# The channel MLP's first two rows computed whole, and its order of products rewritten, in an attention and MLP kernel

## The chip, the core and the metric

The kernel runs on one core of a Trainium2 chip. Its engines are TensorE (PE, with PEld for its weight loads), VectorE (DVE), ScalarE (ACT), GpSimd (POOL) and SyncE (SP, which issues the transfers). The metric is the device time of one execution in microseconds.

## The reference

```python
attn = softmax(q @ k.T / sqrt(D) + bias) @ v                # 4 batches, 8 heads, 576 tokens, 64 wide
x = attn, heads side by side                                # (4, 576, 512)
h = relu(x.T @ w_tok1) @ w_tok2;  u = x + h.T               # token MLP, 256 hidden
y = u + relu(u @ w_ch1) @ w_ch2                             # channel MLP, 1536 hidden
u2, v2 = split(gelu(y @ w_in))                              # gated MLP
out = y + (u2 * (w_sg @ norm(v2) + b_sg)) @ w_out
```

The change is in the channel MLP, and in the last steps of the token MLP ahead of it.

## The kernel before

A float32 operand is split into a high and a low part: ACT copies it to fp32r (the high part), DVE subtracts that from the operand (the low part). A product is three matmuls, high by high, high by low and low by high. X holds the activations, 512 channels in four blocks of 128 by 2304 tokens.

The channel MLP takes the tokens in three parts: tokens 0 to 1023 (pass 0, `d0`), the 256 tokens from 1024 on, along with pass 0 (`up256`, `down256`), and the last 1024 (pass 1, `d1`). The 1536 hidden channels are 12 blocks f, two to a row j. A row is a product of 2x2 blocks: two hidden blocks by two halves of the channels, times two halves of the channels by two halves of 512 tokens. It is computed with seven block products in place of eight, from sums of weight blocks (`wsum`, S1 to S4, made in four pieces by `sum_steps`) and sums of activation blocks, the mixers M1 to M4 and M22. A block product (`product`) is 6 matmuls of 512 columns. The products of a row are here called P1 (bank a, first half of wa by first half of u), P2 (bank b), S2M2 (onto a), S1M1 (bank c), S3M3 (onto a), P4 (M4, onto a), P3 (S4M22, onto c). Each time before bank a is accumulated onto again, ACT copies what it holds (to s1, then c12, then c22, the last two in `slots`). The other four outputs of a row go through relu into g tiles (`gs`, two) and then into the down product with w_ch2 (`down`, 12 matmuls of 512 columns into four banks a0 to a3): `down1` for the first 512 tokens of the pass row by row, and for the other 512 once every two rows, for both rows ("others", four down products) after which `add_up` adds the banks to X on DVE. A row that begins a new pair (rows 2 and 4) carries the others of the pair before it; the last pair's come in a closing part after row 5.

Row 0 of pass 0 is special (`first`): its first output, the relu of pg, is computed whole in the token stage with 12 matmuls; the row then needs six products more.

Weights come as 512 KB transfers into two buffers, and are turned into float32 and split by a queue of jobs (`Jobs`). A job has four pieces: ACT squares one word, DVE does L159, L165, L170 and L175; its high part is copied by ACT in the second piece of the next job and its low part subtracted by DVE in the third (`finish`, `subtract`). In pass 0 each row has five jobs: wa, wq with wb, the row's sums, and two of w_ch2, called c. `work(k)` runs k pieces, `step(k)` runs k pieces, one entry of `builds` (mixers for pass 1), pending low parts of relus and one transposing of the residual (`rfill`). `need` runs as many pieces as it takes for a weight to be ready. `wjobs.limit` holds the queue back until buffers are free. In pass 1 all weights of w_ch1 come back split from memory, and the queue turns the next stage's weights.

All orders are written out by hand; every engine takes its instructions in the order in which the program writes them, and waits where a semaphore tells it to. `bank(nm)` gives one of eight PSUM banks: ma, mb, mx, my and a0 to a3.

Of the kernel before, what the change touches and what calls it, by code (L numbers as in the profile page):

```python
# [19 lines left out]
def kernel(ctx, tc, ins, consts, out, dbg=None, nb=4, stop=None):  # L20
# [5 lines left out]
    P = 128  # L26
# [1059 lines left out]
    if True:  # L1086
# [23 lines left out]
        for b in range(nb):  # L1110
# [19 lines left out]
            for d in range(ND):  # L1130
                next_x(b + 1, d + 1, xs)
                tok2(b, d, h)
                if b == nb - 1 and d < 2 * ND2:
                    b11, b12, b21, b22 = [x[:, d % ND2] for x in quarters(0)]
                    t = tk.tile([P, NS - d % 2, DM], F32, tag=f"x{d % 2}", name="raw")[:, 0]
                    if d < ND2:
                        raw_sum(t, b12, b11)
                        split_to(M1, d, t)
                    else:
# [79 lines left out]
    with tc.tile_pool(name="ps_ch", bufs=1, space=PSUM, reuse_waits="tile") as pc:  # L1219
# [7 lines left out]
        def down(acc, g, f, start, stop):  # L1227
            wjobs.need(("c2", f))
            for d in range(ND):
# [11 lines left out]
        builds, pending = [], []  # L1241
# [12 lines left out]

        def up256(j):

            wjobs.need(("c1", 2 * j + 1))
            pg = bank("mx")
# [8 lines left out]
            relu(pg, gs[0])  # L1267
# [20 lines left out]
        class Double:  # L1288
# [13 lines left out]
            def down1(self, j, e, group):  # L1302
                if self.acc is None:
                    self.acc = new_acc()
                down(self.acc, gs[e], 2 * j + e, j == group[0] and e == 0, j == group[-1] and e == 1)
# [13 lines left out]
            def others_down(self, acc, lst, k):  # L1319
# [4 lines left out]
            def run(self, hooks, first=False, small=False, banks=("mb", "mb"), end=None):  # L1324

                self.small = small
                seq = [(g, j) for g in self.groups for j in g]
                for n, (group, j) in enumerate(seq):
                    pgrp, pj = seq[n - 1] if n > 0 else (None, None)
                    begins = n > 0 and j == group[0]  # L1330
                    direct = first and n == 0
# [5 lines left out]
                    sm = small and n < len(seq) - 1  # L1337
                    hooks(n, "start")
                    a = bank("ma")
                    product(a, self.half(w_a, 0), self.half(self.u, 0), start=True)  # L1340
                    if not direct:
                        S.copy(out=s1, in_=a)
                    step(self.pieces)
                    if direct:
                        self.down1(j, 0, group)
                    elif n > 0 and not (first and n == 1):
                        self.down1(pj, 0, pgrp)
# [3 lines left out]
                    step(self.pieces)  # L1351
                    if begins:
                        self.down1(pj, 1, pgrp)
                        self.close()
                        self.second(0, lst)
                        step(self.pieces)
                    if not direct:
                        b = bank(banks[0])
                        product(b, self.half(w_a, 1), self.half(self.u, 1), start=True)
                        V.tensor_tensor(out=s1, in0=b, in1=s1, op=ALU.add)  # L1360
                    hooks(n, "P2")
                    step(self.pieces)
                    wjobs.need(("sum", j))
                    product(a, ws_(S2), M2)
                    S.copy(out=c12, in_=a)  # L1365
                    step(self.pieces)
                    if sm and n > 0:
                        down256(j)
                    if begins:
                        self.second(1, lst)  # L1370
                    elif not direct:
                        relu(s1, gs[0])
                    step(self.pieces)
                    if begins:
                        acc, h_ = new_acc(), len(lst) // 2
                        for k in range(h_):
                            self.others_down(acc, lst, k)
                            step(self.pieces)
                    c = bank(banks[1])
# [5 lines left out]
                    step(self.pieces)  # L1385
                    if begins:
                        for k in range(h_, len(lst)):
                            self.others_down(acc, lst, k)
                            if not small and k + 2 == len(lst):
                                relu(s1, gs[0])  # L1390
                            if k + 1 < len(lst):
                                step(self.pieces)
                        add_up(acc, self.c0 + CK, range(ND2))
                        if small:
                            relu_hi(s1, gs[0])
                            relu_lo(s1, gs[0])
                        add_up(acc, self.c0 + CK, range(ND2, ND))
# [3 lines left out]
                    elif sm:  # L1401
# [439 lines left out]
```

## Time and profile before

| | us |
|---|---|
| median of 3 runs | 914.03 (913.85 to 915.43) |
| the profiled execution | 914.67, span 912.9 |
| PE, DVE, ACT, POOL busy | 865.9, 703.2, 453.1, 229.3 |
| pass 0 | 359.2 to 563.1 |
| pass 1 | 563.1 to 700.2 |

The span is what the profile covers of the execution. Times in the rows below are in us from its start. A matmul's own duration is longer than the distance to the next one, since matmuls are pipelined; the distance between starts is the pace.

### The profile page before, as it was taken

To read this page: it belongs to the slowest core of one execution; us is meant where nothing else is said; L and a number is where in the kernel's file an instruction comes from. 1 tells how busy PE (TensorE), PEld (TensorE's weight loads), DVE (VectorE), ACT (ScalarE), POOL (GpSimd) and SP (SyncE) were. 2 spreads that over 40 slices of the span, in tenths; PEclk is the share of its full clock that TensorE was granted. 3 is DMA by queue.
4 is the path that set the end of the run, shared out by engine and by line. 5 is a ranking of instruction groups with operands and counts; after the bars stand their busy time and mean duration, and the time that the engine had idled before them with its cause. 6 is when DMAs were issued, how large, how long until landed. Compare 5 with 4: busy or idle time off the path is not lost. (4 is left out here: it accounts for less than half of the span.)

```text
span 912.9 us, 21627 instructions
## 1 busy us (share of the span) xinstructions
PE 865.9 (95%) x8608; PEld 712.3 (78%) x8608; DVE 703.2 (77%) x1531; ACT 453.1 (50%) x993; POOL 229.3 (25%) x440
## 2 busy tenths in 40 slices
PE   9999999999999997888988989999989999999998
PEld 4466788888888886766876767787867999989997
DVE  7899688888887787677767785456485989988856
ACT  7999788888888432333233342123243532323310
POOL 0345576766766000000000000000002232321240
PEclk9999999999999999889999999999989999999999
DMA  7956544444431330135233110325042001000002
GB/s 187 195 125 138 133 79 84 82 88 86 95 77 39 86 113 24 47 104 172 81 116 116 46 47 24 136 84 209 11 107 52 35 24 47 1 34 25 1 13 93
DMA packets 127732, 74.30 MB, mean 81 GB/s; under 512 B 104592, under 2 KB 112912, under 8 KB 126352
## 3 DMA queue, kind: packets, MB, share of 16 engines
q1 hardware_dynamic: 127472, 72.79, 30.1%
q8 instruction: 68, 1.11, 0.5%
q14 instruction: 32, 0.26, 0.1%
q10 hardware_dynamic: 160, 0.13, 0.1%
HBM read 47.01 MB, written 13.11 MB: 66 GB/s over the span
## 5 line engine op out<-in xcount | busy, mean ns | idle before, releaser
L530 POOL TENSOR_SCALAR pr<-pr,sm 128x576 f32<-128x576 f32 (+2 forms) x208 | 129.7, 640 | 47.4 <-DVE sm L523 39.2
L1231 PE MATMUL a<-g,c 128*128 128x512 f32 x528 | 130.9, 401 | 9.2 <-ACT g L1070 5.2
L1231 PEld LDWEIGHTS a<-g,c 128*128 128x128 f32 x528 | 102.0, 195 | 32.8 <-ACT g L1070 5.7
L516 ACT ACTIVATE pr<-pr,mn 128x576 f32<-128x576 f32 x144 | 112.2, 779 | 6.9 <-DVE mn L503 4.6
L503 DVE CUSTOM_DVE_ANT_0 pr<-ss,bias_m 128x576 f32<-128x576 f32 x128 | 94.6, 750 | 19.9 <-PE ss L497 17.0
L63 POOL TENSOR_TENSOR y<-X,y 128x576 fp32r<-128x576 f32 x4 | 5.6, 1426 | 402.5 <-ACT y L62 402.5
L597 PE MATMUL o<-xA,vm 64*64 64x128 f32 (+1 forms) x1280 | 78.8, 261 | 0.0
L597 PEld LDWEIGHTS o<-xA,vm 64*64 64x64 f32 x1280 | 69.9, 133 | 11.1 <-issue 5.4
L1186 DVE STREAM_TRANSPOSE res<-X 32x256 f32<-32x256 f32 (+1 forms) x176 | 68.1, 387 | 2.8
L598 PE MATMUL o<-yA,vm 64*64 64x128 f32 x1024 | 68.0, 272 | 0.0
L497 PE MATMUL ss<-kt,X 64*64 64x288 f32 x816 | 66.8, 410 | 0.0
L598 PEld LDWEIGHTS o<-yA,vm 64*64 64x64 f32 x1024 | 56.3, 133 | 0.3
L1652 PE MATMUL ps<-wsT,vn 128*128 128x288 f32 x384 | 56.4, 295 | 0.0
L374 DVE TENSOR_SCALAR X<-ttab,wsm 128x576 f32<-128x576 f32 x108 | 55.4, 574 | 0.1
L1652 PEld LDWEIGHTS ps<-wsT,vn 128*128 128x128 f32 x384 | 52.7, 188 | 0.3 <-POOL vn L63 0.2
L1630 PEld LDWEIGHTS pu<-y,c 128*128 128x128 f32 x384 | 51.3, 188 | 0.3
L1630 PE MATMUL pu<-y,c 128*128 128x288 f32 x384 | 51.5, 294 | 0.0
L158 ACT ACTIVATE sq<-wraw 128x512 f32<-128x512 f32 (+2 forms) x43 | 27.9, 648 | 41.4 <-DVE w L175 23.4
L573 PE MATMUL x<-ident,pr 128*128 128x128 f32 x320 | 47.0, 273 | 0.0
L1064 PE MATMUL ma<-m,ws 128*128 128x512 f32 x144 | 38.4, 403 | 7.9 <-ACT cs L1365 7.9
L1683 PE MATMUL po<-u,gm 128*128 128x512 f32 x192 | 44.0, 389 | 0.0
L1683 PEld LDWEIGHTS po<-u,gm 128*128 128x128 f32 x192 | 36.0, 188 | 7.4
(239 smaller groups left out, 1975.7 us busy)
## 6 DMA issues: line engine op xcount, KB each, us to landing
wraw<-in_moe_w_ch_dram SPq DMA_DIRECT2D x24, 512.0 KB, 3.7
bias_m<-bst SPq DMA_DIRECT2D x32, 288.0 KB, 4.1
s<-ws SPq DMA_DIRECT2D x5, 1024.0 KB, 4.0
ws<-s SPq DMA_DIRECT2D x5, 1024.0 KB, 5.2
vm<-in_v_dram SPq DMA_DIRECT2D x32, 128.0 KB, 3.1
wraw<-in_moe_w_in_dram SPq DMA_DIRECT2D x8, 512.0 KB, 4.3
out_dram<-res SPq DMA_DIRECT2D x16, 256.0 KB, 2.1
kr<-in_k_dram SPq DMA_DIRECT2D x48, 72.0 KB, 2.7
```

What stands on the lines that cost most here:

```text
L374: V.tensor_scalar(out=hd, in0=tt, scalar1=b1i, scalar2=None, op0=ALU.min)
L497: T.matmul(ss[a % na][o, hf, 0:HN], lhsT=ql, rhs=kr_, start=True, stop=True)
L503: V.tensor_tensor_reduce(out=pr[:, a * NB:a * NB + N].rearrange("p (f n) -> p f n", f=2), in0=ss[a][:, :, 0:HN], in1=bias[a].rearrange("p ...
L516: S.activation(out=pr[:, a * NB:a * NB + N], in_=pr[:, a * NB:a * NB + N], func=AF.Exp, scale=-1.0, bias=mn[:, a:a + 1], accum_out=sm[:, a ...
L530: G.tensor_scalar(out=pr[:, dc:dc + hi - lo], in0=pr[:, lo:hi], scalar1=sm[:, a:a + 1], scalar2=1.0, op0=ALU.mult, op1=ALU.mult,)
L597: T.matmul(o[0:HD, 0:w], lhsT=vm[r, t, 0], rhs=xs[r, t, 0:w], start=st_, stop=en)
L598: T.matmul(o[HD:P, 0:w], lhsT=vm[r, t, 1], rhs=rh[r], start=st_, stop=en)
L1186: V.transpose(out=o, in_=src(c)[32 * a:32 * a + 32])
L1231: T.matmul(acc[d], lhsT=c2[f][i][:, d * P:(d + 1) * P], rhs=g[:, j], start=start and m == 0, stop=stop and m == 2,)
L1630: T.matmul(pu[:, hf, 0:HN], lhsT=wi[i][0][d][:, f * P:(f + 1) * P], rhs=y[j][:, d, js], start=d == 0 and m == 0, stop=d == ND - 1 and m == 2,)
L1652: T.matmul(ps[:, hf, 0:HN], lhsT=vn[i][:, t, ds_], rhs=wsT[j][:, t, js], start=t == 0 and m == 0, stop=False,)
L1683: T.matmul(po[:, cs], lhsT=g[i][:, d, gs], rhs=wo[j][d][:, cs], start=d == 0 and m == 0, stop=d == NG - 1 and m == 2,)
```

## The change

The first two of the twelve rows of hidden blocks, row j = 0 here, are now computed without sums in pass 0: `pair0` makes C12 (bank a), C22 (bank b) and later C21 (bank c) with 12 matmuls each, from the weights and the activations themselves. For that M1 and M2 hold at first the two blocks of u for tokens 512 to 1023, split in the token stage, and the four mixers are built inside `pair0`. The split of the 256 tokens (x256) moves to the token stage. `up256` comes after S2M2 and `down256` after P4, or after the first of the others. A down product can be done in two parts, d 0 and 1, then 2 and 3 (pass 1). The low part of a relu follows at once; only that of the 256 tokens stands apart. In pass 1 bank a is ma and my by turns. Steps have three pieces in pass 0 (two before) and two in pass 1 (three before); builds are called one by one. The split of u0 for the next stage moves from P2 to P4 of the last row.

```diff
-                if b == nb - 1 and d < 2 * ND2:
...
-                        raw_sum(t, b22, b12)
-                        raw_sum(t, t, b11, ALU.add)
-                        split_to(M2, d % ND2, t)
+                if b == nb - 1 and d == 0:
+                    split(quarters(0)[1], *M1)
+                if b == nb - 1 and d == 1:
+                    split(quarters(0)[3], *M2)
+                if b == nb - 1 and d == 2:
+                    x256 = chw.tile([P, 2, ND, CS], F32R, tag="ws1", name="x256")
+                    split(X[:, :, C256:C256 + CS], x256[:, 0], x256[:, 1])
...
         def relu(src, g):
             relu_hi(src, g)
-            pending.append(lambda: relu_lo(src, g))
+            relu_lo(src, g)
 
         def step(k):
             work(k)
-            if builds:
-                builds.pop(0)()
-            while pending:
-                pending.pop(0)()
             rfill(1)
...
+            def other(self, acc, lst, k, n=0):
                 down(acc, self.g(k), lst[k][0], k == 0, k == len(lst) - 1)
                 if k + 2 < len(lst):
                     self.second(k + 2, lst)
+                step(n)
+
+            def pair0(self):
+
+                (j, j1), a, b = self.groups[0], bank("ma"), bank("mb")
+                for ps, w, m in ((a, [wa[j][:, i] for i in range(2)], (M1, M2)), (b, None, (M1, M2))):
+                    for e in range(2):
+                        if w is None:
+                            w2 = [(wq, wb)[e][j][:, i] for i in range(2)]
+                        else:
+                            w2 = self.half(w, e)
+                        product(ps, w2, m[e], start=e == 0)
+                    S.activation(out=slots[0 if w is not None else 1], in_=ps, func=AF.Relu)
+                self.hooks(0, "others")
+                self.down1(j, 0, self.groups[0])
+                up256(j)
+                relu_lo_256()
+                c = bank("ma")
+                for e in range(2):
+                    product(c, [(wq, wb)[e][j][:, i] for i in range(2)], self.half(self.u, e), start=e == 0)
+                relu(c, gs[1])
+                self.hooks(0, "C21")
+                down256(j)
+                self.hooks(0, "P3")
...
+                    k_ = self.pieces
+                    a = bank(banks[n % 2])
                     product(a, self.half(w_a, 0), self.half(self.u, 0), start=True)
+                    S.copy(out=s1, in_=a)
+                    step(k_)
+                    if da:
+                        self.down1(pj, 0, pgrp, range(ND) if small or begins else range(ND2))
+                    step(k_)
+                    if begins:
+                        if not small:
+                            self.second(0, lst)
+                        self.down1(pj, 1, pgrp)
+                        self.close()
+                        if small:
+                            self.second(0, lst)
+                        else:
+                            self.second(1, lst)
+                    b = bank(banks[2])
+                    product(b, self.half(w_a, 1), self.half(self.u, 1), start=True)
+                    V.tensor_tensor(out=s1, in0=b, in1=s1, op=ALU.add)
+                    hooks(n, "P2")
+                    wjobs.need(("sum", j))
+                    product(a, ws_(S2), M2)
+                    S.copy(out=c12, in_=a)
+                    step(k_)
+                    if da and not small and not begins:
+                        self.down1(pj, 0, pgrp, range(ND2, ND))
+                        relu(s1, gs[0])
                     if sm:
                         up256(j)
                         hooks(n, "up")
+                        step(k_ if not begins else 1)
+                        relu_lo_256()
                     if begins:
+                        acc = new_acc()
+                        self.other(acc, lst, 0, k_)
+                        if small:
+                            down256(j)
+                            self.second(1, lst)
+                        else:
+                            self.other(acc, lst, 1, k_)
+                    c = bank(banks[3])
                     product(c, ws_(S1), M1, start=True)
                     product(a, ws_(S3), M3)
                     S.copy(out=c22, in_=a)
                     V.tensor_tensor(out=c22, in0=c, in1=c22, op=ALU.add)
                     hooks(n, "P7")
+                    step(k_)
                     if begins:
+                        for k in range(1 if small else 2, len(lst)):
+                            self.other(acc, lst, k, k_ if k + 1 < len(lst) else 0)
...
+                        add_up(acc, self.c0 + CK)
                         if small:
+                            relu(s1, gs[0])
                         hooks(n, "done")
                     elif n > 0:
                         self.down1(pj, 1, pgrp)
+                        step(1)
                     product(a, [wb[j][:, i] for i in range(2)], M4)
                     relu(a, gs[1])
                     hooks(n, "P4")
+                    if sm and not begins:
+                        down256(j)
+                        relu(s1, gs[0])
+                    elif not sm and not begins and (small or not da):
+                        relu(s1, gs[0])
                     product(c, ws_(S4), M22)
                     V.tensor_tensor(out=c12, in0=c, in1=c12, op=ALU.add)
                     hooks(n, "P3")
...
-        d0.pieces, d1.pieces = 2, 0
+        d0.pieces, d1.pieces = 3, 0
...
+            if n == 0 and where == "others":
+                mixer(3, raws(), 0)
+                for i in range(2):
+                    S.copy(out=M22[i], in_=M2[i].bitcast(F32))
+                mixer(2, raws(), 0)
+            if n == 0 and where == "C21":
+                wjobs.limit = base + 8
+                work(8)
+                mixer(1, slots[2:4], 0)
             if where == "P3":
                 wjobs.limit = base + 5 * (n + 1) + 5
-                work(4)
+                work(4 if n > 0 else 0)
+            if n == 0 and where == "P3":
+                mixer(4, raws(), 0)
...
-                d1.pieces = 3
-            if n == NJ - 1 and where == "P2":
+                d1.pieces = 2
+            if n == NJ - 1 and where == "P4":
                 y0.extend(u_parts(0, u0))
...
-        d1.run(hooks1, banks=("mb", "mx"), end=("mb", "mx", "my", "ma"))
+        d1.run(hooks1, banks=("ma", "my", "mb", "mx"), end=("ma", "mb", "mx", "my"))
```

## Rows read from the trace of the kernel before

**Rows 1.** The page: PE's busy time, and the channel weights' transfers.
```profile
PE 865.9 (95%) x8608; PEld 712.3 (78%) x8608; DVE 703.2 (77%) x1531; ACT 453.1 (50%) x993; POOL 229.3 (25%) x440
...
wraw<-in_moe_w_ch_dram SPq DMA_DIRECT2D x24, 512.0 KB, 3.7
```

**Rows 2.** Busy time by stage: PE, PEld, DVE, ACT, POOL; clock, DMA, GB/s.
```profile
359.20:563.10 203.90, 174.89 (x824) 143.81 (x823) 151.35 (x253) 68.12 (x120) 0.00 (x0) 0.92 0.25 82
563.10:700.17 137.07, 128.12 (x541) 102.28 (x539) 80.19 (x133) 40.59 (x69) 4.85 (x4) 0.98 0.33 102
632.90:658.90 26.00, 26.00 (x115) 21.21 (x113) 11.26 (x17) 5.42 (x9) 0.00 (x0) 1.00 0.22 84
```

**Rows 3.** Timeline of PE: start, us, line, tile, count, in two dense places.
```profile
547.98 1.59 PE L1279 MATMUL my<-g,c 128*128 128x256 f32 x12
549.41 1.60 PE L1279 MATMUL mx<-g,c 128*128 128x256 f32 x12
...
590.68 5.60 PE L1231 MATMUL a<-g,c 128*128 128x512 f32 x24
596.12 1.52 PE L1064 MATMUL mb<-u,wa 128*128 128x512 f32 x6
```

**Rows 4.** Waits of PE, pass 0 then pass 1: total, times, longest, us.
```profile
PE my L1279 <- ACT c L122: 9.7, 7, 1.6
...
PE my L1279 <- DVE c L132: 4.3, 4, 1.2
...
PE ma L1064 <- ACT wa L122: 0.8, 2, 0.4
...
PE ma L1064 <- ACT cs L1365: 5.7, 2, 4.5
...
PE ma L1064 <- ACT cs L1382: 0.7, 1, 0.7
```

**Rows 5.** Timeline of PE, first row, and S2M2 of row 1 (last line).
```profile
365.98 5.22 PE L1231 MATMUL a<-g,c 128*128 128x512 f32 x12 [5.25 <-ACT g L1070]
...
393.66 1.52 PE L1064 MATMUL ma<-m,ws 128*128 128x512 f32 x6
```

**Rows 6.** Timeline of PE: row 1's waits for c; starts behind P1 of rows 2 to 5.
```profile
400.46 2.59 PE L1279 MATMUL my<-g,c 128*128 128x256 f32 x9 [1.39 <-ACT c L122]
...
415.75 2.89 PE L1231 MATMUL a<-g,c 128*128 128x512 f32 x12
...
454.42 2.89 PE L1231 MATMUL a<-g,c 128*128 128x512 f32 x12
...
480.96 2.90 PE L1231 MATMUL a<-g,c 128*128 128x512 f32 x12
...
519.48 2.88 PE L1231 MATMUL a<-g,c 128*128 128x512 f32 x12
```

**Rows 7.** Timeline of DVE: a sum job's ends, add-ups, a weight job's ends, mixer.
```profile
388.50 0.75 DVE L978 TENSOR_TENSOR sq<-w 128x256 f32<-128x256 f32 x2
...
392.28 0.69 DVE L985 TENSOR_TENSOR ws<-sq,ws 128x512 fp32r<-128x512 f32 x1 [0.69 <-ACT ws L981]
...
422.79 2.47 DVE L1239 TENSOR_TENSOR X<-a,X 128x512 f32<-128x512 f32 x4
...
427.78 0.42 DVE L159 TENSOR_SCALAR w<-wraw 128x512 int32<-128x512 int32 x1
...
430.16 0.69 DVE L175 SCALAR_TENSOR_TENSOR w<-sq,w 128x512 f32<-128x512 f32 x1
...
534.22 1.29 DVE L1435 TENSOR_TENSOR m<-scratch,m 128x512 fp32r<-128x512 f32 x2
```

**Rows 8.** Timeline of ACT at the end of the token stage.
```profile
364.81 0.62 ACT L62 CAST m<-raw 128x512 fp32r<-128x512 f32 x1 [2.75 <-DVE raw L1051]
365.34 0.59 ACT L1070 ACTIVATE g<-pg 128x512 fp32r<-128x512 f32 x1
```

**Rows 9.** Timeline of ACT, then of PE, in pass 1's last row.
```profile
665.53 2.18 ACT L62 CAST u<-X 128x512 fp32r<-128x512 f32 x4
...
671.88 2.93 PE L1064 MATMUL ma<-m,ws 128*128 128x512 f32 x6 [4.46 <-ACT cs L1365]
```

More of the change, by code (lines that the diff above doesn't have):

```diff
@@ L1225, in new_acc, with down @@
             return [bank(f"a{d}") for d in range(ND)]
-        def down(acc, g, f, start, stop):
+        def down(acc, g, f, start, stop, ds=range(ND)):
             wjobs.need(("c2", f))
-            for d in range(ND):
+            for d in ds:
                 for m, (i, j) in enumerate(TERMS):
@@ L1266, in up256, with relu_lo_256 @@
                         )
-            relu(pg, gs[0])
+            relu_hi(pg, gs[0])
+        def relu_lo_256():
+            relu_lo(small_pg[0], gs[0])
+        small_pg = [None]
         def down256(j):
@@ L1322, in others_down, with run @@
                     self.second(k + 2, lst)
-            def run(self, hooks, first=False, small=False, banks=("mb", "mb"), end=None):
-                self.small = small
+                step(n)
[20 more added lines that the diff above has]
+                self.hooks(0, "P3")
+            def run(self, hooks, first=False, small=False, banks=("ma", "ma", "mb", "mb"), end=None):
+                self.small, self.hooks = small, hooks
                 seq = [(g, j) for g in self.groups for j in g]
                 for n, (group, j) in enumerate(seq):
+                    hooks(n, "start")
+                    if first and n == 0:
+                        self.pair0()
+                        continue
                     pgrp, pj = seq[n - 1] if n > 0 else (None, None)
                     begins = n > 0 and j == group[0]
-                    direct = first and n == 0
                     pos = 2 * group.index(j)
@@ L1336, in run @@
                     ws_ = lambda o: [wsum[j][:, i, o] for i in range(2)]
-                    sm = small and n < len(seq) - 1
-                    hooks(n, "start")
-                    a = bank("ma")
+                    sm, da = small and n < len(seq) - 1, n > 0 and not (first and n == 1)
+                    k_ = self.pieces
+                    a = bank(banks[n % 2])
                     product(a, self.half(w_a, 0), self.half(self.u, 0), start=True)
[L1341 to L1347, printed above, removed]
+                    S.copy(out=s1, in_=a)
[23 more added lines that the diff above has]
+                        relu(s1, gs[0])
                     if sm:
@@ L1350, in run @@
                         hooks(n, "up")
-                    step(self.pieces)
+                        step(k_ if not begins else 1)
+                        relu_lo_256()
                     if begins:
[L1353 to L1379, printed above, removed]
+                        acc = new_acc()
[6 more added lines that the diff above has]
+                    c = bank(banks[3])
                     product(c, ws_(S1), M1, start=True)
@@ L1405, in run @@
                     hooks(n, "P4")
-                    step(0 if begins else self.pieces)
+                    if sm and not begins:
[3 more added lines that the diff above has]
+                        relu(s1, gs[0])
                     product(c, ws_(S4), M22)
@@ L1409, in run @@
                     hooks(n, "P3")
+                    if not small:
+                        step(1)
                 group, j = seq[-1]
                 lst = self.others(group)
+                build()
                 self.down1(j, 0, group)
+                build()
                 if small:
                     up256(j)
-                step(self.pieces)
+                    relu_lo_256()
+                else:
+                    self.second(0, lst)
+                    step(self.pieces)
                 self.down1(j, 1, group)
                 self.close()
-                self.second(0, lst)
-                step(self.pieces)
                 if small:
+                    self.second(0, lst)
                     down256(j)
@@ L1425, in run @@
                 for k in range(len(lst)):
-                    self.others_down(acc, lst, k)
-                    if k + 1 < len(lst):
-                        step(self.pieces)
+                    self.other(acc, lst, k, self.pieces if k + 1 < len(lst) else 0)
+                    build()
                 add_up(acc, self.c0 + CK)
@@ L1478, in hooks0 @@
                 for i in (3, 2, 4, 1):
-                    builds.append(lambda i=i: mixer(i, [scratch[:, d] for d in range(ND2)], D1))
+                    builds.append(lambda i=i: mixer(i, raws(), D1))
                 builds.append(lambda: split(quarters(D1)[3], *M22))
```

44 lines of the change are left out of this document (11 added, 33 removed).

## The prediction

> **What bounds the kernel now.** The page first: PE is busy 95% of the span [rows 1], so at a glance little can be had. The second view, busy time by stage, says where to look. The channel stage is two passes, pass 0 (359.2 to 563.1 us) and pass 1 (563.1 to 700.2). In pass 0 PE is busy 174.89 of 203.90 us at a granted clock of 0.92, in pass 1 128.12 of 137.07 at 0.98, and in the stretch 632.9 to 658.9 all of 26.00 at 1.00 [rows 2]. So a dense stretch exists with the same instructions, and the others can be measured against it.
>
> The pace there: 24 matmuls of 512 columns start in 5.44 us, 0.2267 each, so a block product of 6 is 1.36 and a down product of 12 is 2.72; 12 of 256 columns start in 1.43 us, 0.1195 each [rows 3]. By the code pass 0 has 246 + 288 of the wide ones and 288 narrow ones, pass 1 252 + 288 wide ones (the counts of [rows 2], but for three that belong to the stages beside). Dense, that is 121.1 + 34.4 = 155.5 and 122.4 us. So 48.4 us of pass 0 are lost, and 13.9 of the 136.3 that pass 1 takes to its last down product. The wait view names the causes [rows 4]: weights of the second product (c) that ACT and DVE have not yet split when the 256 tokens' down product wants them; the c12 copy on ACT; small waits for wa.
>
> Losses by place, from the start times [rows 5, 6] less the dense work between them: first row with the second's P1, P2 and S2M2, 359.20 to 395.02: 35.8 - 23.6 = 12.2. Rest of row 1, to 415.75: 20.7 - 12.4 = 8.3. Row 2, to 454.42: 38.7 - 31.6 = 7.1. Row 3, to 480.96: 26.5 - 20.7 = 5.8. Row 4, to 519.48: 38.5 - 31.6 = 6.9. Row 5 and the closing part, to 563.12: 43.6 - 35.7 = 7.9. With pass 1's 13.9: 62.1 us.
>
> A wait costs more than its length: after 5.25 us of idling, 12 matmuls took 5.22 us where the dense pace is 2.72 [rows 5]. That is the lower clock, 1.2 in place of 2.4 GHz, and 2.5 us on top. So busy PE time holds loss as well. By busy time alone 29.0 + 9.0 = 38.0 us were to be had; by counting, 62.1. The Trainium skill (Perfetto Trace Analysis, Identifying the Most-Contended Engine) calls matmul busy time a bad measure of the distance to the roofline and sends the reader to LDWEIGHTS busy share. By that share, 21.21 of 26.00 in the dense stretch against 143.81 + 102.28 here [rows 2], the two passes would shrink to 301.6 us and 39.4 us were to be had; that reading is the third rival below.
>
> **The change, part by part.** No product is added or dropped: the first rows take 8 block products before and after. What moves is DVE and ACT work, and PE's order.
>
> *Prices on DVE* [rows 7]: a weight job is about 2.5 us in four pieces (427.78 to 430.85 less another's low half, 0.6, that lies within), and its low half 0.6 more; a sum job (four pieces) 388.50 to 392.97, 4.5; four add-ups 2.5; one mixer 1.3 for the low parts and about as much for the differences, with ACT's casts between; a relu's low part 0.6.
>
> *First two rows.* The difference-and-split chains leave the token stage; relu of pg no longer stands behind four casts on ACT, each of which waits for a DVE difference [rows 8], so the 5.25 us and its 2.5 of clock go. In their place PE runs a, b (5.44), down (2.72), up256 (2.87), C21 (2.72), down256 (2.87), P1 and P2 of row 1 (2.72) without a wait that I can find: from 359.2 to 378.5. But DVE now gets the four mixers in the same stretch. Its first two fit behind a and b. From C21's end at 373.0: relu 1.3 (374.4), wa's low half and the last two pieces of the open job 1.9 (376.3), sum 1 4.5 (380.8), mixer 1 2.5 (383.3), two add-ups of down256 1.2 (384.5), differences of mixer 4 1.25 and their last cast on ACT (386.4). Only then comes ACT's copy of P1 to s1 (387.0), because it is written behind those casts, and S2M2 accumulates onto the bank that this copy reads. So PE idles 378.5 to 387.0, 8.5 us, plus 2.5 of clock: 11.0 lost against 12.2. A big part of the edit gives almost nothing, 1.2. Queued behind that copy on ACT: the row's weight squares and casts; nobody else waits earlier than PE. Bounds: 0 lost if DVE or ACT runs ahead of this order (no row shows such a thing), 16 if every mixer also waits a cast of 0.6 twice. I take 11.0.
>
> *Second product of the 256 tokens late.* It is now after P4 (rows 1, 3) or after the first other-half down product (rows 2, 4), and three pieces per step instead of two. Rows 1 and 3: between S2M2 and down256 PE has up256, two products, a down product and P4, 9.7 us. DVE comes to s1's add-up 9.5 after the row's start (below), 2.7 after S2M2's end; five pieces and a low half (3.7) later c is split, at 6.4, and after two more pieces the 256 tokens' relu is done, at 8.4. No wait, by 1.3 us; 8.3 and 5.8 gained. If that cover is short by as much, row 3 pays it whole. Rows 2 and 4: on DVE after the P3 add-up stand sum 4.5, first c job 2.5, two pieces 1.1, add-ups 2.5, a relu and s1 1.2, then 5 pieces and two relus 4.4, then the low half 0.6: 16.8, from 0.8 after the row's start, so 17.6. PE reaches down256 after P1, two down products, P2, S2M2, up256 and a down product: 15.1. So 2.5 us of wait and some 0.3 at the row's end (relu behind four add-ups): 2.8 each, against 7.1 and 6.9; 4.3 and 4.1 gained. Bounds: 0, and the full 7.
>
> *Row 5 and the close.* The c jobs end inside row 5. But no up256 stands between P2 and S1M1, which share bank mb: s1's add-up comes 0.8 + 4.5 + 2.5 + 1.1 + 0.6 = 9.5 after the row's start, S1M1 could start at 6.8: 2.7 lost, and 0.9 where the s1 relu follows four splits of u. 3.6 against 7.9; 4.3 gained. The builds go out between down products; DVE ends them before pass 1's P1.
>
> *Pass 1.* Half a down product (1.36) between S2M2 and S1M1, banks ma and my taking turns, and the split of u0 for the next stage moved from P2 to P4. Before, four casts (2.18) [rows 9] stood ahead of the c12 copy, and S3M3 waited 4.46 at 671.88 and then ran at half pace (2.93 for 6, and more after). All of that goes, as does the other wait of this kind, 1.2 [rows 4]. What stays: 0.7 in its first row, where no down product lies between S3M3 and P4 [rows 4], and an estimated 0.4 before the second of the last four down products. 1.1 against 13.9; 12.8 gained. Bounds: 5 gained if the four splits late in the last row push the close's relus back, 13.9.
>
> *Split parts of a down product, relu's low half at once instead of at the next step, 128x1024 splits, copies to M22 on ACT:* nothing on PE's path; they hide under down products. DVE saves some 3 us in the first row.
>
> Sum: 1.2 + 8.3 + 4.3 + 5.8 + 4.1 + 4.3 + 12.8 = 40.8. Off this 2.0 for five row starts at 0.4, since wa's low half comes late at two row starts now [rows 4] and every row now starts earlier for DVE. 38.8. The profiled execution took 914.67, so 875.9; the median of the runs shown is 0.64 below it: 875.2, and I say 875.
>
> **The rivals.** (1) *DVE becomes the bound of pass 0.* For: 151.35 us busy there [rows 2]; in 175.5 us that is some 148, 84%, with ACT in between at each split. Against: no chain of the walk above ends later than the product that it feeds in rows 1 and 3. If each of rows 1 to 5 waits 3 us more: 890. (2) *Pass 1's loss only moves* to its close, 5 of 12.8 gained: 883. (3) *Only idle time comes back.* Busy time would then be all work at its own pace: 38.0 us idle now, and of my list 8.5 + 5 + 2.7 + 0.9 + 1.1 + 2.0 stay, 20.2, so 17.8 gained: 896. It speaks against this that the dense stretch runs the same instructions at 0.2267 and the slow ones follow idling [rows 3, 5]; the LDWEIGHTS share of the skill's page gives the same size. (4) *Slower:* PE never gets its full clock back in pass 0, because waits of 2 to 3 us now stand in each row. Half clock adds 0.2267 to a wide matmul, so 172 of them at half clock beyond those now eat the 38.8 us; more than that and it is slower, with all 534 wide ones at half clock some 996. Against: granted 0.92 even with today's waits. (5) *Nothing changes:* the weights' transfers set the pace; but 20 loads at 3.7 us [rows 1] are 74 us in a 175 us pass.
>
> **How the numbers follow.** Forecast 0.60, (1) 0.19, (2) 0.10, (3) 0.05, (4) 0.03, (5) 0.03. A change under 0.2% (1.8 us) could not be told from none here. Faster 0.94, same 0.03, slower 0.03. Range: down to 866, where the 8.5 us of the first row are not waited for; up to 890, rival 1. Forecast's own range is 866 to 882.
>
> **What would show it.** After: pass 0 some 175 us and pass 1 some 124; one PE wait near 8 us before row 1's S2M2, released by the s1 copy on ACT; waits for c only in rows 2 and 4, under 3 us; no wait for a c12 copy near pass 1's end. It would be wrong if ACT or DVE is held by a chain that the walk above does not see, above all in row 1, where the jobs are all behind by the first rows' mixers.

## The result, and the profile after

| | before | after |
|---|---|---|
| median, us | 914.04 (913.85 to 915.43) | 880.48 (878.13 to 882.52) |
| the profiled execution | 914.67, span 912.9 | 878.13, span 876.3 |
| pass 0 | 359.2 to 563.1 | 358.3 to 537.1 |
| pass 1, to its last down product | 563.1 to 699.4 | 537.1 to 661.35 |

The ratio is 0.963 (95% interval 0.960 to 0.966): 33.6 us faster, where 39 were forecast.

The page after, PE first: busy time fell by 17.2 us with the same 8608 matmuls [rows 1], so about half of the 36.6 us between the spans is pace, not idle time.

```profile
PE 848.7 (97%) x8608; PEld 704.3 (80%) x8608; DVE 698.6 (80%) x1526; ACT 457.0 (52%) x996; POOL 231.8 (26%) x440
```

Busy time by stage after (columns as in [rows 2]): pass 0, pass 1, then three parts of pass 0, the last of which reaches 3 us into pass 1.

```profile
358.32:537.12 178.80, 162.79 (x825) 136.88 (x823) 144.72 (x245) 68.84 (x121) 0.00 (x0) 0.97 0.28 93
537.12:661.35 124.23, 123.15 (x541) 101.04 (x539) 78.17 (x131) 40.72 (x69) 2.76 (x2) 1.00 0.32 103
376.00:440.00 64.00, 54.01 (x272) 45.35 (x271) 55.19 (x97) 24.44 (x45) 0.00 (x0) 0.95 0.43 140
440.00:500.00 60.00, 57.90 (x297) 48.81 (x295) 50.89 (x89) 22.86 (x41) 0.00 (x0) 1.00 0.33 110
500.00:540.00 40.00, 36.09 (x171) 29.57 (x170) 30.73 (x49) 15.40 (x26) 0.00 (x0) 0.96 0.08 27
```

Idle time in the two passes went from 37.2 to 17.1 us and busy time from 303.0 to 285.9. (The 38.0 that [rows 2] give run 0.8 us further, to the start of the next stage's first product.) Pass 1 is now almost dense: 124.2 us for 122.4 of matmuls. In pass 0 most of the loss sits in two places, around 376 to 440 and after 500; between them PE idles 2.1 us in 60 at full clock, in row 4.

PE's waits in pass 0 after (columns as in [rows 4]), then the one at the handover, which is here the end of pass 1 and the next stage's first product, pv.

```profile
PE ma L1064 <- ACT s L1370: 8.3, 1, 8.3
PE mb L1064 <- DVE s L1386: 2.3, 1, 2.3
PE my L1281 <- DVE c L132: 1.8, 2, 0.9
PE a L1228 <- ACT c L122: 1.3, 1, 1.3
...
PE pv L1615 <- DVE X L1236: 2.3, 1, 2.3
```

The 9.7 and 4.3 us for c and the 5.7 for the c12 copy [rows 4] are gone but for 1.8 + 1.3; in rows 2 and 4 waits of 1.9 in all for the 256 tokens' relu have come in. The forecast 8.5 us before row 1's S2M2 are there, at 8.3, released by the s1 copy, and so are the 2.7 before row 5's S1M1, at 2.3. The timeline of PE at these two places, and at the handover:

```profile
376.40 1.52 PE L1064 MATMUL mb<-u,wa 128*128 128x512 f32 x6
386.23 2.93 PE L1064 MATMUL ma<-m,ws 128*128 128x512 f32 x6 [8.30 <-ACT s L1370]
388.95 1.97 PE L1260 MATMUL mx<-x,wa 128*128 128x256 f32 x12
...
502.55 2.92 PE L1064 MATMUL mb<-m,ws 128*128 128x512 f32 x6 [2.27 <-DVE s L1386]
...
520.12 3.38 PE L1228 MATMUL a<-g,c 128*128 128x512 f32 x12 [1.25 <-ACT c L122]
...
663.60 11.22 PE L1615 MATMUL pv<-c,u 128*128 128x512 f32 x48 [2.25 <-DVE X L1236]
```

Six matmuls that take 1.52 on the first line take 2.93 behind the 8.3 us wait, and in this execution 2.92 behind a wait of only 2.27: the price of the short wait is then more than its length.

Losses by place, counted as in the prediction (start to start, less dense work; in us). The first place also starts 0.9 earlier. The starts behind P1 of rows 2 to 5, as in [rows 6], and that of pass 1:

```profile
404.64 5.60 PE L1228 MATMUL a<-g,c 128*128 128x512 f32 x24
...
439.06 2.88 PE L1228 MATMUL a<-g,c 128*128 128x512 f32 x12
...
459.82 5.60 PE L1228 MATMUL a<-g,c 128*128 128x512 f32 x24
...
494.67 2.89 PE L1228 MATMUL a<-g,c 128*128 128x512 f32 x12
...
537.12 1.52 PE L1064 MATMUL ma<-u,wa 128*128 128x512 f32 x6
```

| place | before | forecast | after |
|---|---|---|---|
| row 0 to row 1's S2M2 | 12.2 | 11.0 | 9.9 |
| rest of row 1 | 8.3 | 0 | 0.4 |
| row 2 | 7.1 | 2.8 | 2.8 |
| row 3 | 5.8 | 0 | 0.1 |
| row 4 | 6.9 | 2.8 | 3.3 |
| row 5 and close | 7.9 | 3.6 | 6.8 |
| pass 1 | 13.9 | 1.1 | 1.8 |

37.0 and the 0.9 are gained; the wait at the handover, 0.8 before, takes 1.5 back. That makes 36.4 of the 36.6 us between the two spans.

### The profile page after: what moved, and what is told of

It reads as the page before. It is cut to its first block, busy times and chain, and to the rows that moved or that the text cites. A ratio compares the mean times of both kernels' runs of the same rounds, so it can differ in the third digit from the quotient of the medians.

```text
span 876.3 us, 21629 instructions
## 1 busy us (share of the span) xinstructions
PE 848.7 (97%) x8608; PEld 704.3 (80%) x8608; DVE 698.6 (80%) x1526; ACT 457.0 (52%) x996; POOL 231.8 (26%) x440
## 4 chain that ended last, share of the span: by engine, by line
PE 53%; DVE 7%; ACT 2%; issue 1%; DMA 0%; DVEq 0%; ACTq 0%; SPq 0%
PE a L1228 11%; PE ps L1690 6%; PE pu L1668 6%; PE pv L1615 6%; PE po L1721 6%; PE ma L1064 5%; PE mb L1064 3%; PE my L1064 2%; PE mx L1064 2%; PE pu L1099 2%; PE mx L1260 1%; PE ph L674 1%; DVE g L1074 1%; DVE X L1236 1%; PE mx L1281 1%; DVE w L170 1%
## 5 line engine op out<-in xcount | busy, mean ns | idle before, releaser
L1228 PE MATMUL a<-g,c 128*128 128x512 f32 x528 | 125.7, 390 | 1.6 <-ACT c L122 1.3
L1228 PEld LDWEIGHTS a<-g,c 128*128 128x128 f32 x528 | 98.7, 188 | 23.1 <-ACT c L122 1.5
L63 POOL TENSOR_TENSOR gm<-uT,gm 128x512 fp32r<-128x512 f32 x16 | 23.3, 1454 | 70.0 <-ACT gm L62 70.0
```

The costliest lines, as they stand in the source:

```text
L1228: T.matmul(acc[d], lhsT=c2[f][i][:, d * P:(d + 1) * P], rhs=g[:, j], start=start and m == 0, stop=stop and m == 2,)
```

## Experiments

The theory: the gain is the sum of the waits that went, each with the clock behind it, and most of it is the late second product of the 256 tokens and pass 1's half down product; what it fell short by is row 5's s1 wait, the handover, and a clock that comes back at different times from run to run. Rivals: DVE, not the ACT copy, holds rows 0 to 2, so that shortening the 8.3 us gains nothing; the banks that take turns, or the late split of u0, do pass 1's work; the first rows' edit does more than the 1.2 us that it was given. The kernel before ran beside each group at 914.1 to 915.0, and every edit is made to the changed kernel.

**The changed kernel again.** No edit.

> The changed kernel again, as the yardstick for the others of this job. Its four runs so far went from 878.1 to 882.5 us with mean granted clocks from 0.994 down to 0.986. Theory A (the spread is the clock: after the 8.3 us wait of PE before row 1's S2M2 and the waits in row 5 the clock comes back sooner in some executions than in others): again 878 to 883, and the time falls in step with the granted clock. Theory B (spread of transfers): spread without relation to the clock.

879.71 (877.87 to 883.11). The profiled one took 883.11, and its waits are those of the profile after within 0.1 us. What differs is the clock; here the same stretches as above, and PE behind the same 8.3 us:

```profile
376.00:440.00 64.00, 54.00 (x263) 45.64 (x263) 53.50 (x92) 23.70 (x43) 0.00 (x0) 0.89 0.43 140
440.00:500.00 60.00, 57.84 (x290) 49.11 (x289) 50.08 (x90) 21.66 (x39) 0.00 (x0) 0.97 0.33 110
```
```profile
386.11 2.93 PE L1064 MATMUL ma<-m,ws 128*128 128x512 f32 x6 [8.31 <-ACT s L1370]
388.83 2.49 PE L1260 MATMUL mx<-x,wa 128*128 128x256 f32 x12
```

0.89 against 0.95, and 2.49 us against 1.97 for the same 12 matmuls. Over the nine executions of this kernel the mean clock goes with the time: 877.9 to 878.4 at 0.991 to 0.994, 882.5 to 883.1 at 0.986. So between these two traces the difference is how soon the full clock returns behind equal waits; of the other seven executions only the mean clock is known. The Trainium skill (TensorE: Matmul & The Clock Gate, What's actually happening) says that the number of matmuls at the lower clock differs between runs of one kernel. It speaks of a kernel's start; these two traces show the like behind a wait.

**Mixer 4 later.** Its DVE and ACT work goes behind the s1 copy and the P2 add-up.

```diff
-            if n == 0 and where == "P3":
+            if n == 1 and where == "P2":
                 mixer(4, raws(), 0)
```

> Mixer 4 is built after row 1's copy to s1 (at row 1's P2) in place of the end of the first rows. Theory A (S2M2 of row 1 waits for the s1 copy, which stands on ACT behind mixer 4's casts, 385.6 in the profile; the row's sums are there at 380.1): the copy comes after mixer 1's casts, at about 382, PE's wait falls from 8.3 to 4 to 5 us and the lower clock behind it shortens by up to 1; 3 to 5 us faster than the changed kernel, some 876. Rival B (DVE is the bound of these rows, so 2.6 us of mixer work only moves behind): the wait shows up again at row 1's down256 or S3M3, and the time stays within 1 us.

880.0 (878.2 to 880.0): no gain that stands out from the spread, though the wait shrank from 8.3 to 4.5.

```profile
381.85 2.93 PE L1064 MATMUL ma<-m,ws 128*128 128x512 f32 x6 [4.53 <-ACT s L1370]
...
420.17 1.10 PE L1281 MATMUL my<-g,c 128*128 128x256 f32 x7 [0.90 <-DVE c L132]
```

Row 2's last wait for c ends at 420.17 where it ended at 421.35 (below): PE came 4.4 us earlier to S2M2 and got through here 1.2 earlier, of which 0.6 are an earlier start of pass 0. The rest went in short waits (0.40 at 396.45, 0.30 at 414.08; 0.93, where it was 0.39, at row 2's down256) and in matmuls at the lower clock.

**Mixers 1 and 4 later.** As above, with mixer 1 as well.

```diff
-                mixer(1, slots[2:4], 0)
...
-            if n == 0 and where == "P3":
+            if n == 1 and where == "P2":
+                mixer(1, slots[2:4], 0)
                 mixer(4, raws(), 0)
```

> Mixers 1 and 4 are both built at row 1's P2. Theory A: S2M2 waits only for the row's sums (about 380.1) and the wait falls to some 2.3 us, but then S1M1 waits for mixer 1, which DVE now builds after six weight pieces and s1's add-up, some 3 us; 4 to 7 us faster than the changed kernel, 874 to 877. Rival B (DVE-bound): same as the changed kernel within 1 us, the wait before S2M2 being replaced by one of the same size before S1M1.

879.56 (878.9 to 881.3): no gain either, with S2M2's wait at 1.9. Waits of 1.1 for mixer 1 and 1.5 for the c12 copy came in, and row 2's wait for c ends at 420.55. The first rival holds here: from C21's relu on, DVE is the chain. Its timeline in the changed kernel, first and last of 68 lines, and PE's line that waits for the last:

```profile
372.98 0.69 DVE L1074 SCALAR_TENSOR_TENSOR g<-ma,g 128x512 fp32r<-128x512 f32 x1 [2.05 <-ACT g L1070]
...
420.61 0.68 DVE L132 TENSOR_TENSOR c<-w,c 128x512 fp32r<-128x512 f32 x1
```
```profile
421.35 1.10 PE L1281 MATMUL my<-g,c 128*128 128x256 f32 x7 [0.90 <-DVE c L132]
```

In the 48 us between, waits of DVE add up to 2.9. Its work there can be put in another order, but row 2's down256 waits for all of it.

**Row 5's s1 first.** In row 5 of pass 0 the queue's pieces come after S2M2, not before P2's add-up.

```diff
-                    step(k_)
+                    last0 = small and not sm
+                    step(0 if last0 else k_)
                     if da:
...
-                    step(k_)
+                    step(0 if last0 else k_)
                     if begins:
...
                     S.copy(out=c12, in_=a)
-                    step(k_)
+                    step(3 * k_ if last0 else k_)
```

> In pass 0's last row the six weight pieces that stand between the s1 copy and the s1 add-up on DVE are run after S2M2. Theory A (S1M1 waits 2.3 us for the bank that the s1 add-up reads, and another 1.7 us go to the lower clock behind it): both go, 3 to 4 us faster than the changed kernel, 876 to 877. Rival B (the pieces only come later, and the last c weights are waited for in down1 of the close, 1.25 us now): within 1 us, with that wait grown by some 3.

875.77 (874.5 to 879.1), 4 us less than the changed kernel beside it. Where S1M1 waited, PE now runs through:

```profile
498.76 1.52 PE L1064 MATMUL ma<-m,ws 128*128 128x512 f32 x6
500.12 1.52 PE L1064 MATMUL mb<-m,ws 128*128 128x512 f32 x6
501.48 1.52 PE L1064 MATMUL ma<-m,ws 128*128 128x512 f32 x6
```

S3M3 starts at 501.48 where it started at 505.28: 3.8 us for a wait of 2.27. The wait of 1.3 in the close stays, one of 0.3 for the s1 relu grows to 1.0, and pv starts 3.4 earlier.

The price of that wait is not the same in every execution. Eight traces have it, at 2.27 or 2.28. In four of them (the profile after, the changed kernel again, mixer 4 later, one bank) S1M1 and S3M3 behind it take 1.7 us longer than dense; in the other four 0.1 to 0.2, as in the next run:

```profile
528.42 1.66 PE L1064 MATMUL mb<-m,ws 128*128 128x512 f32 x6 [2.27 <-DVE s L1386]
```

**The 256 tokens' second product early again**, right behind up256; everything else stays.

```diff
                         relu_lo_256()
+                        down256(j)
...
-                            down256(j)
...
                     if sm and not begins:
-                        down256(j)
                         relu(s1, gs[0])
```

> The 256 tokens' second product stands right behind their first again (rows 1 and 3: before S1M1; rows 2 and 4: before the first of the others); all else as in the changed kernel. Theory A (the gain of rows 1 to 4 comes from moving this product behind work that does not need the new c weights): PE waits for the 256 tokens' relu and for c in every row, some 5.5 us in rows 1 and 3 and 5 in rows 2 and 4 besides the lower clock, so 12 to 22 us slower than the changed kernel, 892 to 902. Rival B (three pieces per step and relus at once did it): within 4 us of the changed kernel.

903.25 (902.0 to 904.1): 22 to 24 us slower than the changed kernel, up to 2 more than expected. The waits, and the ends of rows 1 to 4 counted as in the table:

```profile
PE my L1281 <- ACT g L1070: 10.0, 4, 3.3
PE ma L1064 <- ACT s L1370: 8.3, 1, 8.3
PE my L1281 <- DVE g L1074: 5.4, 2, 2.8
PE a L1228 <- ACT g L1070: 2.7, 2, 1.3
```
```profile
388.76 2.56 PE L1260 MATMUL mx<-x,wa 128*128 128x256 f32 x12
...
520.54 2.88 PE L1228 MATMUL a<-g,c 128*128 128x512 f32 x12
```

They are no longer for c but for the 256 tokens' relu, which with three pieces a step stands behind more weight work. So it is distance in PE's order that pays. But this order is not that of the kernel before, where P2 and S2M2 stood between up256 and down256: rows 1 to 4 lose 32.7 us here, 28.1 before and 6.6 after. The run shows that the place of down256 is worth much in the changed kernel; it doesn't show which share of the 21.5 us gained in these rows is due to it, and which to three pieces a step and the relus' low parts at once.

**One bank in pass 1.**

```diff
-        d1.run(hooks1, banks=("ma", "my", "mb", "mx"), end=("ma", "mb", "mx", "my"))
+        d1.run(hooks1, banks=("ma", "ma", "mb", "mx"), end=("ma", "mb", "mx", "my"))
```

> In pass 1 bank a is ma in every row again (no turns with my). Theory A (half a down product between S2M2 and S1M1 gives the copies their time; turning banks saves only the short wait at a row's start, for a relu's low part): up to 1 us slower than the changed kernel, with waits of 0.1 to 0.2 us at row starts. Rival B (the turning banks are what took pass 1's loss away): 5 to 12 us slower.

881.0 (878.6 to 883.7), with the same waits: the banks that take turns are worth nothing that shows beside a spread of 5 us.

**The split of u0 early again.**

```diff
-            if n == NJ - 1 and where == "P4":
+            if n == NJ - 1 and where == "P2":
                 y0.extend(u_parts(0, u0))
```

> The split of u0 for the next stage stands at P2 of pass 1's last row again. Theory A (half a down product and S1M1, 2.7 us, now lie between the c12 copy's source and S3M3, and hide the four casts of 2.2 us): within 1 us of the changed kernel, perhaps with the 2.3 us wait at the next stage's start shorter, since DVE is freer at the end. Rival B (the early split was the cause of the 4.46 us wait, whatever lies between): S3M3 waits 2 to 4 us again, plus lower clock, 3 to 6 us slower.

881.34 (876.7 to 883.3): the same. ACT's four casts stand ahead of the c12 copy again, and no wait comes of it, since half a down product now lies between; the lines of ACT and PE, against [rows 9]:

```profile
632.15 2.17 ACT L62 CAST u<-X 128x512 fp32r<-128x512 f32 x4
634.23 0.57 ACT L1390 COPY cs<-my 128x512 f32<-128x512 f32 x1
...
634.93 1.57 PE L1064 MATMUL my<-m,ws 128*128 128x512 f32 x6
```

Of the three edits that the prediction names in pass 1 the half down product is then the one left that can have brought the gain. It was not undone by itself, nor were the new places of steps and relus in pass 1, so this is argued and not shown.

**First rows as before**, in the token stage's end and in `pair0` (six products from sums, mixers 1 and 2 split in the token stage); the other rows as changed.

```diff
-                if b == nb - 1 and d == 0:
-                    split(quarters(0)[1], *M1)
...
+                    if d < ND2:
+                        raw_sum(t, b12, b11)
+                        split_to(M1, d, t)
...
+                product(a, ws_(S2), M2)
+                S.copy(out=c12, in_=a)
+                step(4)
+                c = bank("mb")
+                product(c, ws_(S1), M1, start=True)
...
+            if n == 0 and where == "mix":
+                mixer(2, slots[2:4], 0, False)
+                mixer(4, slots[2:4], 0)
```

> The first two rows as before (sums, S2M2 and so on, mixers M1 and M2 built in the token stage), all later rows as changed. Theory A (the prediction's: that part of the edit is worth about 1 us, since a wait of 5.3 us before the first down product only turns into one of 8.3 before S2M2): 1 to 3 us slower than the changed kernel, some 882. Theory C (DVE is the bound from the first rows' end to row 2's down256, as the two runs with later mixers suggest, and the edit takes 3 us of DVE work away and starts it earlier): 3 to 5 slower. Rival B (the first rows' edit carries much of the gain): 8 or more slower.

885.19 (883.8 to 888.7), 4 us slower than the two runs just above, on the same chip. The start of that stretch on PE, and row 1's S2M2:

```profile
359.36 1.55 PE L1064 MATMUL ma<-u,wa 128*128 128x512 f32 x6
366.15 5.05 PE L1231 MATMUL a<-g,c 128*128 128x512 f32 x12 [5.23 <-ACT g L1070]
...
392.79 1.96 PE L1064 MATMUL ma<-m,ws 128*128 128x512 f32 x6 [1.86 <-ACT s L1385]
394.55 2.76 PE L1263 MATMUL mx<-x,wa 128*128 128x256 f32 x12
```

From 359.36 to 394.55 it takes 35.2 us for the same 20.7 of dense work that the changed kernel does in 30.6 from 358.32 on. The loss is 14.5, not the 12.2 of before, since row 1's up256 now comes after S2M2 and no longer stands between P1 and it: the s1 copy is waited for here too. So by this trace the first rows' edit is worth 4.6 and 1.0 of earlier start, by the medians some 4 in all, but only beside the new order of the rows.

**Three pieces in pass 1**, on top of row 5's s1 first, for the handover.

```diff
-                d1.pieces = 2
+                d1.pieces = 3
```

> The kernel with the s1 add-up first in pass 0's last row (875.8 us), and three pieces per step in pass 1 in place of two. Theory A (the next stage's first product waits 2.25 us for X because the last two weight pieces, in front of the add-ups on DVE, run at 1.9 and 1.8 us instead of 0.7 while GpSimd subtracts for y; with three pieces they are done before): the wait falls to 0.8 us as in the kernel before, some 1.5 us faster, 874 to 875. Rival B (the add-ups themselves come late whatever stands before them, as X is read by the y casts): the wait stays at 2.2 us and the time the same within 1 us.

875.12 (873.2 to 876.5). The 2.25 us ahead of pv are gone, but a wait in pass 1's close grew from 0.41 to 1.64. The median is 0.65 us below that of row 5's edit alone, less than either run's spread, so no net gain is shown.

```profile
654.11 0.73 PE L1228 MATMUL ma<-g,c 128*128 128x512 f32 x2 [1.64 <-DVE g L1074]
...
662.18 4.02 PE L1616 MATMUL pv<-c,u 128*128 128x512 f32 x17
```

**The mixers' differences on GpSimd**, on top of row 5's s1 first, with two pieces in pass 1.

```diff
+        def g_sum(o, x, y, op=ALU.subtract):
+            G.tensor_tensor(out=o, in0=x, in1=y, op=op)
...
-                mixer(3, raws(), 0)
+                mixer(3, raws(), 0, True, g_sum)
```

and the same for mixers 2, 1 and 4.

> The kernel with the s1 add-up first (875.8 us), and the eight differences of the first rows' mixers computed by GpSimd, idle there, in place of DVE. Theory C (DVE has no idle time from the end of C21 to row 2's down256, and sets both the wait before row 1's S2M2 and the one in row 2): 2.5 us of DVE work go from that chain, the S2M2 wait falls from 8.3 to 5 to 6 us, row 2's product comes 2 us earlier, 1.5 to 3 us faster, 873 to 874. Rival D (GpSimd and DVE slow each other, as at the next stage's start where DVE took 1.9 us in place of 0.7): DVE loses as much as it is given, and the time stays or grows by up to 3.

878.47 (876.2 to 879.0): not faster than 875.8. Yet S2M2 waits 5.1 and row 2's wait for c ends at 418.44, 2.9 earlier than in the changed kernel (0.8 of it because pass 0 starts earlier). About half of that goes at once to the lower clock: from there to the next S1M1 it takes 3.75 us, where it took 2.37. Most of the rest is lost at the handover: pv starts at 660.11, after 3.47 of waiting for DVE, where with row 5's edit alone it started at 660.22, after 2.24. And DVE is slower beside GpSimd, 1.41 us for an instruction that takes 0.65 in [rows 7]:

```profile
367.46 2.82 DVE L1472 TENSOR_TENSOR m<-scratch,m 128x512 fp32r<-128x512 f32 x2 [1.85 <-ACT m L1470]
```

**All three together.** The two edits above on row 5's.

> The three edits together (s1 add-up first, three pieces in pass 1, mixer differences on GpSimd). By theories A and C their gains add, as they lie in different stages: 871 to 873 us. By rivals B and D: 875 to 879.

872.89 (872.3 to 873.7), ratio 0.955 (0.953 to 0.956): the fastest, 7 us below the changed kernel. Against the run with three pieces and no GpSimd, on the same chip, the median is 2.2 lower, though with four executions each the spread of that run (873.2 to 876.5) reaches into this one's. Row 2's wait for c ends at 419.07, 2.3 earlier than in the changed kernel with the same start, and pv starts at 658.71 without a wait: with the handover clear, what rows 0 to 2 gain reaches the end.

**Filler matmuls.** On all three: 16 matmuls by a tile of zeros, in the wait before row 1's S2M2, to hold the clock up there.

```diff
+                    if first and n == 1:
+                        for i in range(16):
+                            T.matmul(
+                                self.acc[i % ND], lhsT=zt, rhs=self.u[0][:, 0], start=False, stop=False,
+                                skip_group_check=True,
+                            )
```

> The kernel with the three edits (872.9 us, 872.3 to 873.7), and 16 matmuls that add products of a block of zeros to the down banks, put into PE's 5.0 us wait before row 1's S2M2 (3.6 us of work that changes no value). Theory A (a wait costs its length and then the lower clock behind it): S2M2 runs at the full pace, 1.36 us in place of 2.73, and the products after it too; the wait shrinks to about 1.4 and nothing else moves, 1.5 to 2.5 us faster, near 871. Rival B (DVE's chain sets row 2's product, so PE only arrives there earlier and waits longer): within 0.7 us, with row 2's waits longer by what S2M2 gains. Rival C (the filler delays S2M2): slower.

873.9 (five executions from 871.9 to 874.4; the profiled one took 4763 us, so there is no trace to read): no gain. The mean clock of the five was 0.996 to 0.999, against 0.994 to 0.996 without the filler, so PE seems to have kept a little more of it. That DVE's chain took the time back, as in the runs with later mixers, would fit but is not shown.

## Why the prediction came out as it did

**The method held.** Counting starts against a dense pace said 62.1 us were to be had where idle time said 38.0. The kernel gained 36.6 in its span, with 25 still lost by the same count. In the two passes idle time gave 20.1 and busy time 17.1: the third rival (only idle time comes back, 896) is out. The Trainium skill (Perfetto Trace Analysis, Identifying the Most-Contended Engine) names the LDWEIGHTS busy share as a measure of how close a kernel is to the roofline. The prediction read it as a ceiling of 39.4 us for the two passes (39.3 when worked out again), and this is just passed: with all three edits they take 300.4 us, from 358.36 to 658.71, 39.8 below the 340.2 of before. Nor was it a fixed floor: PEld's busy time fell from 246.1 to 238.5 us for the same loads.

**Rows 1 to 4** came out at 6.6 us lost against 5.6 forecast. That 16.8 us of DVE work against 15.1 of PE work leaves some 2.5 us of wait in rows 2 and 4 was the right sum: c is there 18.0 after row 2's start, where 17.6 was forecast. That the product's late place matters is shown by the run that puts it early; how the 21.5 us divide between it and the other edits of these rows is not.

**The first rows** waited 8.3 against 8.5, on the instruction named. But the reason beside it (the copy stands behind mixer 4's casts) is only the near end of it: with these out of the way the time did not change. The first rival's mechanism, DVE as the bound, holds for rows 0 to 2 (with some 2.5 us of that chain's work moved to GpSimd, row 2's wait ends 2.3 earlier) but not behind them, where PE idles 2.1 us in 60; the 3 us in each row that it was priced at did not come. The size, 1.2, was too small: 2.3 and 0.9 of start by place, 4 to 5 when undone by itself. The step that failed took before's 12.2 as what the old first rows would cost in the new order; there they cost 14.5.

**Row 5 and the close** are the term that was mis-sized most: 3.6 forecast, 6.8 measured. The wait before S1M1 was named to within 0.5 us (2.27 for 2.7) but booked without the clock behind it, although the prediction had said that a wait costs more than its length; with the slower matmuls it cost 4.1 in this execution. The run without it has S3M3 3.8 earlier. The s1 relu cost 0.7 for 0.9. And the prediction said that the c jobs end inside row 5, but in the close PE waits 1.25 for a c, which with the slower matmuls behind it cost 1.9 and was in no term.

**Pass 1** came out at 1.8 against 1.1, and the second rival (its loss only moves to the close, 883) at 0.4 us there. But one step later it has its like: DVE's pieces for the next stage run into the last add-up, on which pv waits. That handover was in no term: 1.5 us.

**The allowance** of 2.0 for row starts was not needed.

So from 38.8 to 36.6 by place: 3.2 more in row 5 and the close, 1.5 at the handover, 1.6 in rows 1, 4 and pass 1, against 2.0 less in the first rows and the 2.0 of allowance. That they cancel in part is luck. The other part of the miss is that the median lies 2.35 above the profiled execution, where the forecast took it 0.64 below. The kernel before spread over 2.2 us in nine executions beside the changed kernel's five, which spread over 5.2: now waits in rows 0 to 5 leave the clock's return to chance, by 1.7 us or 0.1 at a single wait. The fourth rival had the mechanism, with too high a price to see its small form.

## What to carry to other kernels

A short wait on PE is to be booked with the pace behind it, and as a range: 2.3 us of waiting cost some 4.1 in half of the traces here, and 2.6 in the other half. A consumer late in PE's own order can be worth more than faster producers: putting one product early again cost 22 to 24 us, while moving work off the instruction that releases a wait gave nothing that could be measured, as the same engine's queue feeds the next product too. To learn what a shortened wait is worth, look at where the next wait on the same engine ends, before and after; and clear the last such place (here the handover) first, or part of the gain upstream is given back there.

## Hardware seen on the way

DVE's instructions got slower beside GpSimd when both inputs are in SBUF. At the handover after, GpSimd's four y operations and DVE's pieces:

```profile
658.59 7.02 POOL L63 TENSOR_TENSOR y<-X,y 128x576 fp32r<-128x576 f32 x4 [366.01 <-DMA wsr<-in_moe_w_sg_dram]
```
```profile
658.00 0.69 DVE L165 SCALAR_TENSOR_TENSOR w<-wraw,w 128x512 int32<-128x512 int32 x1
658.61 0.69 DVE L132 TENSOR_TENSOR c<-w,c 128x512 fp32r<-128x512 f32 x1
659.21 1.93 DVE L170 SCALAR_TENSOR_TENSOR w<-wraw,w 128x512 int32<-128x512 int32 x1
661.17 1.77 DVE L175 SCALAR_TENSOR_TENSOR w<-sq,w 128x512 f32<-128x512 f32 x1
662.87 0.68 DVE L1236 TENSOR_TENSOR X<-ma,X 128x512 f32<-128x512 f32 x1
```

L170 and L175 take 1.93 and 1.77 where [rows 7] has 0.69 for the second; the add-up, one of whose inputs is in PSUM, keeps its 0.68. L132, which starts with GpSimd's first, keeps its 0.69 too, though it has two inputs in SBUF. The 2.3 us that L170 and L175 lose (L170 takes 0.68 to 0.69 in rows 0 to 2) are about what pv waits. The Trainium skill (SBUF — State Buffer, Who interferes with whom) says that a DVE instruction with two SBUF inputs contends with a GpSimd instruction that reads SBUF, and one with a single SBUF input, outside its two-port modes, does not. L170 and L175 agree with the first part and the add-up with the second; L132 shows no slowing.
